# Attention values on 64x64 quarters of the matmul array, one query tile at a time, in a one-core attention and MLP kernel

## The chip, the cores and the metric

One core of a Trainium2 chip runs the whole program. The metric is the device time of one execution in microseconds (us). The kernel before took 914.94 us (median of three runs, 913.29 to 915.36).

## The reference, cut to what matters

```python
scores = scale * np.matmul(q, k.transpose(0, 1, 3, 2))      # q, k, v: 4 batches, 8 heads, 576 positions, 64 wide
psi_rel = np.log1p(np.abs(pos[:, None] - pos[None, :]))
psi_i = np.log1p(np.maximum(pos[:, None], 1.0))
h = np.maximum((psi_rel / psi_i)[..., None] @ w1 + b1, 0.0) # 32 hidden numbers for each pair of positions
scores = scores + (h @ w2).transpose(2, 0, 1)[None]         # one bias table per head, the same for all batches
attn = softmax(scores)
x = concatenated heads of np.matmul(attn, v)                # 4 x 576 x 512
...
x = two token and channel mixing MLPs of x                  # not touched by the change
```

Everything is fp32; the MLPs' weights and activations are split into two parts and multiplied in three terms.

## The kernel before, in words

The order on every engine is the order in which the program is written. The first 345 us are attention; the rest, the two MLPs, is not touched.

**Units.** `units` (lines 168 to 173) lists 80 units of work. A unit is one batch, one pair of heads and one tile of queries. Four tiles have 128 queries; the fifth, called the tail tile, has 64, and there both heads share one tile of 128 rows. Batch 0 comes first, by query tile (tail tile first); batches 1 to 3 follow, pair by pair.

**The loop** (line 659) is a pipeline over `n`. One turn issues, in this order: the scores of unit n+3 (`scores`, line 443, four 64x64 quarters of the array at once), the division by the softmax sums for unit n+2 (`normalise`, on POOL and DVE), the transposes of unit n (`turn`, line 510: tiles `x` and `y` for the 512 main keys of the two heads, and `z` for the 64 tail keys of both), in batch 0 the transpose of a query tile (`q_turn`) and the product of two groups of the bias table (`bias_product`), and late in the turn the values of unit n-1 (`values`, line 534). ACT copies `x` (line 516), takes one exp of unit n+3 (line 475), copies `z` (line 528) and takes the other exp; DVE adds the bias (`tensor_tensor_reduce`, line 464) and copies `y` (line 532).

**Values** (line 534) form, for one unit, the product of the transposed probabilities with v: eight matmuls of 128 rows by 64 columns of the array (two side by side, one for each head), then two 64x64 matmuls for the tail keys. The result lies in one PSUM bank, tag `o`; DVE copies it into `X` (`place`, line 436). For pairs 4 to 13 (`paired`, line 500) `values2` (line 556) takes two units of 128 queries together, 256 columns at a time, in two halves that stand in different turns; their transposed probabilities need a second set of buffers, which lies in room kept for later weights (`rooms`, lines 748 to 750).

**PSUM.** Eight banks: two tiles of two banks for scores and bias products (`s_tile`, line 328), and one bank each for the tags `x`, `y`, `z` and `o`.

**The front.** The bias table is made on the chip in 36 groups of 16 query rows, tail queries first (`groups`, line 169). A group is a DVE and ACT step (`hidden`, line 310), a matmul (`bias_product`, line 358), an ACT copy into `st` and a DMA that deals the rows out (`bias_place`, line 371). For main queries the 16 rows of a group go to every eighth partition of `bias_m`; for tail queries they go to 16 neighbouring partitions of `bias_t`, in two DMAs:

```python
D.dma_start(out=bias_m[i0 % P // 16:P:GT, i0 // P], in_=st)                  # line 381
D.dma_start(out=bias_t[a * TL + r0:a * TL + r0 + 16], in_=st[a:P:2])         # line 385
```

Main queries are therefore dealt over the partitions in the same way (`dealt`, `rows`, `place`); tail queries are not. All DMAs are issued by one queue, SP, in program order; `load_v` (line 251) is four of them for a pair of heads, and in batch 0 pairs 0 to 3 are loaded in turns -2 to 1 (`NV`, line 203).

Of the kernel before, what the change touches and what calls it, by code (L numbers as in the profile page):

```python
# [7 lines left out]
F32 = mybir.dt.float32  # L8
F32R = mybir.dt.float32r
I32 = mybir.dt.int32  # L10
AF = mybir.ActivationFunctionType
ALU = mybir.AluOpType
# [7 lines left out]
def kernel(ctx, tc, ins, consts, out, dbg=None, nb=4, stop=None):  # L20
    nc = tc.nc
    V, S, G, T, D = nc.vector, nc.scalar, nc.gpsimd, nc.tensor, nc.sync
# [3 lines left out]
    P = 128  # L26
# [173 lines left out]
    ND0, WN = 2, 512  # L200
    NQ = 2
    TD, QD = 1, 2
    NV = (-2, -1, 0, 1)
    zero = first.tile([P, N], F32, tag="st", name="zero", bufs=4)[:, 0:WN]
    V.memset(zero, 0.0)
    z0 = ps_t.tile([P, WN], F32, tag="x", name="z0")
# [164 lines left out]
    def bias_place(gi, ps):  # L371
        if gi in early:
            st = early.pop(gi)
        else:
            st = first.tile([P, N], F32, tag="st", name="bst", bufs=4)
        S.activation(
            out=st.rearrange("p (a n) -> p a n", a=2), in_=ps[:, :, 0:HN], func=AF.Identity, scale=1.0 / scale, bias=evb
        )
        i0 = 16 * gi
        if i0 < NM * P:  # L380
            D.dma_start(out=bias_m[i0 % P // 16:P:GT, i0 // P], in_=st)
        else:
            r0 = i0 - NM * P
            for a in range(2):
                D.dma_start(out=bias_t[a * TL + r0:a * TL + r0 + 16], in_=st[a:P:2])

    def k_parts0(p, pool, tag):

# [27 lines left out]
    def q_out(n, z):  # L416
        b, p, it = units[n]
        if b > 0:
            return
        w = P if it < NM else TL  # L420
        t = hl_p.tile([P, P], F32, tag="q0", name="q0", bufs=5)[:, 0:w]
        if it < NM:
            S.copy(out=rows(t), in_=dealt(z[:, 1]))
        else:
            S.copy(out=t, in_=z[:, 1, 0:w])
        queries[n] = t

    def dealt(x):  # L430
        return x.rearrange("p (t j s) -> p t s j", j=GT, s=P // GT)

    def rows(x):
        return x.rearrange("p (t s j) -> p t s j", j=GT, s=P // GT)

    def place(p, c0, o):

        V.tensor_copy(
            out=X[:, p, c0:c0 + o.shape[1]].rearrange("p (t j s) -> p t j s", j=GT, s=P // GT),
            in_=o.rearrange("p (t s j) -> p t j s", j=GT, s=P // GT),  # L440
        )

    def scores(n):
        b, p, it = units[n]
# [48 lines left out]
    def slots(flat):  # L493
        x, y, z = flat
        x, y = [t.rearrange("p (s t n) -> p s t n", s=2, t=NM) for t in (x, y)]
        return x, y, z.rearrange("p (s n) -> p s n", s=2)

    rooms = [slots(flatA)]

    def paired(n):  # L500

        return NP <= n // NS < len(pairs) - 2

    def room(n):
        if not paired(n):
            return rooms[0], n % 2
        it = units[n][2]
        return (rooms[0], it) if it < 2 else (rooms[1], 1 if it == NM else it - 2)

    def turn(n, pr, z):  # L510
        b, p, it = units[n]
# [22 lines left out]
    def values(n):  # L534
        b, p, it = units[n]
        vm, vt = vraw[b, p]
        (xs, ys, zs), s_ = room(n)
        xs, ys, zs = xs[:, s_], ys[:, s_], zs[:, s_]
        o = ps_t.tile([P, P], F32, tag="o", name="o")
        w = P if it < NM else TL  # L540
        for t in range(NM):
            T.matmul(o[0:HD, 0:w], lhsT=vm[:, t, 0], rhs=xs[:, t, 0:w], start=t == 0, stop=False)  # L542
            rh = ys[:, t] if it < NM else xs[:, t, TL:P]
            T.matmul(o[HD:P, 0:w], lhsT=vm[:, t, 1], rhs=rh, start=t == 0, stop=False)
        T.matmul(o[0:HD, 0:w], lhsT=vt[0:TL, 0], rhs=zs[0:TL, 0:w], start=False, stop=True)
        lh, rh = (vt[TL:P, 1], zs[TL:P]) if it < NM else (vt[0:TL, 1], zs[0:TL, TL:P])
        T.matmul(o[HD:P, 0:w], lhsT=lh, rhs=rh, start=False, stop=True)
        c0 = b * N + it * P
        if it < NM:
            place(p, c0, o)  # L550
        else:
            V.tensor_copy(out=X[:, p, c0:c0 + w], in_=o[:, 0:w])

    open_o = []

    def values2(n, half):

        b, p, it = units[n]
        vm, vt = vraw[b, p]
        xs, ys, zs = room(n)[0]  # L560
        if half == 0:
            open_o.append(ps_t.tile([P, 2 * P], F32, tag="o", name="o"))
        o = open_o[0]
        for t in range(2 * half, 2 * half + 2):
            T.matmul(o[0:HD], lhsT=vm[:, t, 0], rhs=xs[:, :, t], start=t == 0, stop=False)  # L565
            T.matmul(o[HD:P], lhsT=vm[:, t, 1], rhs=ys[:, :, t], start=t == 0, stop=False)
        if half == 0:
            return
        T.matmul(o[0:HD], lhsT=vt[0:TL, 0], rhs=zs[0:TL], start=False, stop=True)
        T.matmul(o[HD:P], lhsT=vt[TL:P, 1], rhs=zs[TL:P], start=False, stop=True)  # L570
        c0 = b * N + it * P
        place(p, c0, open_o.pop())


    early_v, late_v = {}, {}
    for n in range(U):
        if not paired(n):
            (early_v if n == U - 2 else late_v).setdefault(n + 1, []).append((values, n))
    for F in range(U0, U - 2 * NS, NS):
        late_v.setdefault(F + 2, []).append((values2, F, 0))  # L580
        late_v.setdefault(F + 3, []).append((values2, F, 1))
        early_v.setdefault(F + 4, []).append((values, F + 2))
        late_v.setdefault(F + 5, []).insert(0, (values2, F + 3, 0))
        late_v.setdefault(F + 5 if F + NS == U - 2 * NS else F + 6, []).insert(1, (values2, F + 3, 1))

    def form(l):
        for f, *a in l:
            f(*a)

    HP, TW = 1, 1  # L590
    GALL = len(groups)
    GUP = TL // 16 + 2
    hs = {}

    def hide(gi):
        if gi < GALL:
            hs[gi] = hidden(groups[gi])
# [25 lines left out]
            q_out(u, z)  # L623
    bias_place(groups[GUP - 1], bps)
    gnext = GUP

    def x_part(b, t, xs, px):

# [30 lines left out]
    for n in range(-3, U + 1):  # L659
# [7 lines left out]
            normalise(*st[n + 2])  # L667
        if len(gs) > 0:
            hide(gs[0] + 2)
        z = ps_t.tile([P, 2, P], F32, tag="z", name="z") if n < U else None  # L670
        form(early_v.pop(n, []))
        if n == U - 1:
            early_x([NM])
        if 0 <= n < U:
# [28 lines left out]
        for m in range(NP, len(pairs)):  # L703
            F = NS * m
            if n == F - KT:
                k_turn(*pairs[m])
            if n == F - QT:
                qt_, qr_, M = turned(*pairs[m]), qraw.pop(pairs[m]), NM * P
                V.transpose(
                    out=qt_[:, 0:M].rearrange("p (t s j) -> p t j s", j=GT, s=P // GT),  # L710
                    in_=qr_[:, 0:M].rearrange("p (t j s) -> p t j s", j=GT, s=P // GT),
                )
                V.transpose(out=qt_[:, M:N], in_=qr_[:, M:N])
        if len(gs) > 1:
            bias_place(groups[gs[1]], bp[1])
            if late_e:
# [10 lines left out]

        for p in range(NP):
            if n == NV[p]:
                load_v(0, p, *((raw_p, "") if p < 2 else (first, "x")))  # L730
        if n >= 0 and n % NP == 0 and n // NP + 2 < NS:
            load_q0(order0[n // NP + 2])
        for m in range(NP, len(pairs)):
# [7 lines left out]
        if n == U0:  # L741
            first.release()
            stg = tc.alloc_tile_pool(name="stg", bufs=1, side="right", reuse_waits="tile")
            tokw = tc.alloc_tile_pool(name="tokw", bufs=1, side="right", reuse_waits="tile")
            wjobs = Jobs(stg, 2)
            t1 = [tokw.tile([P, NS, TOK], F32R, name=f"t1{i}") for i in range(2)]

            rb = tokw.tile([P, 2 * NTT * N], F32, tag="t2", name="rb")
            cut = [0, 2 * NM * P, 4 * NM * P, 4 * NM * P + 2 * P]
            rooms.append(slots([rb[:, cut[i]:cut[i + 1]] for i in range(3)]))  # L750
            t2 = []
            for j in range(NM // 2):
                wjobs.add(
                    ("t1", j), "moe_w_tok1", slice(2 * j * P, (2 * j + 2) * P), slice(0, TOK), 2,
                    lambda j=j: [t[:, 2 * j:2 * j + 2, :] for t in t1],
                )
            wjobs.add(
                ("t1", NM // 2), "moe_w_tok1", slice(NM * P, N), slice(0, TOK), 1,
                lambda: [t[:, NM, :] for t in t1], 2,
            )  # L760
            for j in range(NTT):
                for hf in range(2):
                    js = slice(hf * HN, (hf + 1) * HN)
                    wjobs.add(
                        ("t2", j, hf), "moe_w_tok2", slice(j * P, (j + 1) * P), js, 1,
                        lambda j=j, js=js: [t[:, j, js] for t in t2],
                    )
            wjobs.load()
# [1 line left out]
            if wjobs.next <= NM // 2 or wjobs.gen is not None:  # L770
                wjobs.piece()
        if n == U - 2 * NS + 2:
            r = tokw.tile([P, 2, NTT, N], F32R, tag="t2", name="t2")
            t2 += [r[:, i] for i in range(2)]
        if n >= U - 2 * NS + 2:
            for _ in range(WP[1]):
# [573 lines left out]
```

## Time and profile before

| what | value |
|---|---|
| median of three runs | 914.94 us (913.29 to 915.36) |
| the profiled execution, its own time | 913.72 us |
| its span | 911.9 us |
| busy: TensorE, DVE, ACT, POOL | 894.5, 625.6, 394.0, 293.7 us |
[...]
| chain that ended last, by engine | TensorE 78%, DVE 16%, issue 2%, ACT 2%, DMA 2% |

Times in the rows count from the start of the span. PE is TensorE's matmuls and PEld its weight loads; an fp32 matmul shows as two passes, each with its own load, so the program's eight score matmuls are 16 rows. The mode of a matmul, as 64*64, is the piece of the array that it uses; pieces of one mode work at the same time. "idle before <-" gives how long the engine had stood and what ended it.

### The profile page before, as it was taken

Reading aid. Unit: us, or ns where it says so; the run is one execution under the profiler, and the core shown is the slowest. Engines: PE = TensorE matmul, PEld = TensorE weight load, DVE = VectorE, ACT = ScalarE, POOL = GpSimd, SP = SyncE. Lnnn points to the kernel's source line nnn. Section 1 sums busy time; section 2 is a strip of 40 time slices with the busy share of each in tenths; the row PEclk is TensorE's granted clock in tenths of the full one; section 3 lists DMA queues with packets and bytes.
Section 4 is the critical chain, followed back from the end, with each engine's and each line's share of the span. In section 5 each row is a group of like instructions: output and inputs, shape, how many; then the busy total and the mean of one; then the engine's idle time right before and its main releaser. Section 6 shows DMA issues by size and latency. Waiting matters only on the chain.

```text
span 911.9 us, 18151 instructions
## 1 busy us (share of the span) xinstructions
PE 894.5 (98%) x7018; PEld 749.8 (82%) x7018; DVE 625.6 (69%) x1371; ACT 394.0 (43%) x875; POOL 293.7 (32%) x430
## 2 busy tenths in 40 slices
PE   8799999999999999999999999999999999999998
PEld 3366776665666789899999999999999989889996
DVE  6799777887877769988834343232215999896756
ACT  6799766676666754433312121211114532222310
POOL 2366455555545532233310100100002452423230
PEclk9999999999999999999999999999999999999999
DMA  8775534333332113223400100000041001010002
GB/s 157 161 155 118 115 64 94 54 66 68 56 64 56 29 60 93 94 93 121 133 24 24 38 33 24 24 24 1 1 77 48 24 1 47 1 59 1 1 13 92
DMA packets 118966, 54.87 MB, mean 60 GB/s; under 512 B 100832, under 2 KB 107616, under 8 KB 118880
## 3 DMA queue, kind: packets, MB, share of 16 engines
q1 hardware_dynamic: 118880, 53.72, 24.7%
q8 instruction: 55, 0.90, 0.4%
q14 instruction: 31, 0.25, 0.1%
HBM read 38.36 MB, written 4.72 MB: 47 GB/s over the span
## 4 chain that ended last, share of the span: by engine, by line
PE 78%; DVE 16%; issue 2%; ACT 2%; DMA 2%; SPq 0%; DVEq 0%; ACTq 0%
PE a L985 14%; PE pg L822 14%; PE ss L456 9%; PE x L515 5%; PE o L565 4%; PE po L1202 4%; PE pv L1096 4%; PE ps L1171 4%; PE o L542 3%; PE y L520 3%; PE bps L363 3%; PE pu L1149 3%; DVE res L940 2%; DVE w L131 2%; PE pu L854 1%
## 5 line engine op out<-in xcount | busy, mean ns | idle before, releaser
L488 POOL TENSOR_SCALAR pr<-pr,sm 128x576 f32<-128x576 f32 (+2 forms) x208 | 129.1, 637 | 118.8 <-DVE sm L482 114.2
L985 PE MATMUL a<-g,c 128*128 128x384 f32 x864 | 162.4, 335 | 1.8 <-DVE X L993 1.0
L985 PEld LDWEIGHTS a<-g,c 128*128 128x128 f32 x864 | 150.9, 188 | 3.5 <-ACT g L828 2.2
L829 DVE SCALAR_TENSOR_TENSOR g<-pg,g 128x384 fp32r<-128x384 f32 x72 | 40.0, 556 | 163.7 <-ACT g L828 163.7
L822 PE MATMUL pg<-u,c 128*128 128x384 f32 x720 | 134.5, 334 | 0.0
L822 PEld LDWEIGHTS pg<-u,c 128*128 128x128 f32 x720 | 125.6, 188 | 0.1
L828 ACT ACTIVATE g<-pg 128x384 fp32r<-128x384 f32 x72 | 35.3, 490 | 192.2 <-PE pg L822 192.2
L475 ACT ACTIVATE pr<-pr,mn 128x576 f32<-128x576 f32 x144 | 112.0, 778 | 6.9 <-DVE mn L464 6.0
L464 DVE CUSTOM_DVE_ANT_0 pr<-ss,bias_m 128x576 f32<-128x576 f32 x128 | 91.3, 750 | 29.8 <-PE ss L456 29.2
L456 PE MATMUL ss<-kt,X 64*64 64x288 f32 x864 | 77.1, 412 | 0.0
L940 DVE STREAM_TRANSPOSE res<-X 32x256 f32<-32x256 f32 (+1 forms) x176 | 68.1, 387 | 2.8
L60 POOL TENSOR_TENSOR c<-w,c 128x512 fp32r<-128x512 f32 x24 | 35.5, 1479 | 88.9 <-ACT c L59 78.7
L60 POOL TENSOR_TENSOR wi<-w,wi 128x512 fp32r<-128x512 f32 x8 | 14.0, 1754 | 153.0 <-DVE g L829 112.5
L320 DVE TENSOR_SCALAR X<-ttab,wsm 128x576 f32<-128x576 f32 x108 | 62.3, 639 | 0.0
L515 PEld LDWEIGHTS x<-ident,pr 128*128 128x128 f32 x320 | 33.6, 141 | 30.4 <-POOL pr L488 18.9
L1171 PE MATMUL ps<-wsT,vn 128*128 128x288 f32 x384 | 56.5, 296 | 1.1 <-DVE tmp L1181 1.1
L456 PEld LDWEIGHTS ss<-kt,X 64*64 64x64 f32 x864 | 36.6, 132 | 22.3 <-DVE sm L482 7.3
L1171 PEld LDWEIGHTS ps<-wsT,vn 128*128 128x128 f32 x384 | 52.7, 189 | 1.9 <-DVE tmp L1181 1.8
L120 ACT ACTIVATE sq<-wraw 128x512 f32<-128x512 f32 (+2 forms) x43 | 27.9, 648 | 57.5 <-DVE w L136 56.3
L515 PE MATMUL x<-ident,pr 128*128 128x128 f32 x320 | 52.5, 286 | 0.0
L1149 PEld LDWEIGHTS pu<-y,wi 128*128 128x128 f32 x384 | 51.4, 188 | 0.3
L1149 PE MATMUL pu<-y,wi 128*128 128x288 f32 x384 | 51.6, 295 | 0.0
(188 smaller groups left out, 1760.0 us busy)
## 6 DMA issues: line engine op xcount, KB each, us to landing
wraw<-in_moe_w_ch_dram SPq DMA_DIRECT2D x24, 512.0 KB, 3.5
bias_m<-bst SPq DMA_DIRECT2D x32, 288.0 KB, 3.7
vm<-in_v_dram SPq DMA_DIRECT2D x32, 128.0 KB, 2.8
wraw<-in_moe_w_in_dram SPq DMA_DIRECT2D x8, 512.0 KB, 3.4
out_dram<-res SPq DMA_DIRECT2D x16, 256.0 KB, 2.0
kr<-in_k_dram SPq DMA_DIRECT2D x48, 72.0 KB, 2.4
qr<-in_q_dram SPq DMA_DIRECT2D x48, 72.0 KB, 2.4
wraw<-in_moe_w_out_dram SPq DMA_DIRECT2D x4, 512.0 KB, 3.6
```

The source lines that it names most:

```text
L60: (eng or V).tensor_tensor(out=lo, in0=src, in1=hi.bitcast(F32), op=ALU.subtract)
L320: V.tensor_scalar(out=hd, in0=tt, scalar1=b1i, scalar2=None, op0=ALU.min)
L456: T.matmul(ss[a % na][o, hf, 0:HN], lhsT=qt[r, m * HD:(m + 1) * HD], rhs=kt[r, js], start=True, stop=True)
L464: V.tensor_tensor_reduce(out=pr[:, a * NB:a * NB + N].rearrange("p (f n) -> p f n", f=2), in0=ss[a][:, :, 0:HN], in1=bias[a].rearrange("p ...
L475: S.activation(out=pr[:, a * NB:a * NB + N], in_=pr[:, a * NB:a * NB + N], func=AF.Exp, scale=-1.0, bias=mn[:, a:a + 1], accum_out=sm[:, a ...
L488: G.tensor_scalar(out=pr[:, dc:dc + hi - lo], in0=pr[:, lo:hi], scalar1=sm[:, a:a + 1], scalar2=1.0, op0=ALU.mult, op1=ALU.mult,)
L515: T.transpose(x[:, t], pr[:, t * P:(t + 1) * P], ident)
L822: T.matmul(pg, lhsT=c1[f][i][:, d], rhs=u[j][:, d], start=d == 0 and n == 0, stop=d == ND - 1 and n == 2)
L940: V.transpose(out=o, in_=src(c)[32 * a:32 * a + 32])
L985: T.matmul(acc[d], lhsT=c2[f][i][:, d * P:(d + 1) * P], rhs=g[j], start=f == f0 and n == 0, stop=f == f1 and n == 2,)
L1149: T.matmul(pu[:, hf, 0:HN], lhsT=wi[i][:, d, f * P:(f + 1) * P], rhs=y[j][:, d, js], start=d == 0 and m == 0, stop=d == ND - 1 and m == 2,)
L1171: T.matmul(ps[:, hf, 0:HN], lhsT=vn[i][:, t, ds_], rhs=wsT[j][:, t, js], start=t == 0 and m == 0, stop=False,)
```

## The change

It does six things. (1) `values` works on 64x64 quarters: each 128-row matmul is two of 64 rows, and the two halves of the rows add up in two PSUM banks, tag `o` and tag `z`, which is also the tag of the tail keys' transposes. (2) `place` adds the two banks: ACT copies the second into `X`, DVE adds the first. (3) `values2` and its second room go; every unit is formed alone. (4) From unit 11 on, the values of unit n-2 stand in turn n straight behind the scores of unit n+3, ahead of the transposes; up to unit 10 they stay late in the turn. The values of unit 78 follow those of unit 77 in turn 79. (5) Tail queries are dealt like main ones: the 16 rows of a group go to every fourth partition of `bias_t`. (6) In batch 0 v of pairs 0 and 1 is loaded ahead of the loop, that of pairs 2 and 3 in turns -3 and -2.

```diff
-    NV = (-2, -1, 0, 1)
+    NV = (None, None, -3, -2)
...
-                D.dma_start(out=bias_t[a * TL + r0:a * TL + r0 + 16], in_=st[a:P:2])
+                D.dma_start(out=bias_t[a * TL + r0 // 16:(a + 1) * TL:TL // 16], in_=st[a:P:2])
...
-    def place(p, c0, o):
-
-        V.tensor_copy(
-            out=X[:, p, c0:c0 + o.shape[1]].rearrange("p (t j s) -> p t j s", j=GT, s=P // GT),
-            in_=o.rearrange("p (t s j) -> p t j s", j=GT, s=P // GT),
-        )
+    def place(p, c0, os, w):
+
+        out = X[:, p, c0:c0 + w].rearrange("p (j s) -> p j s", s=16)
+        a, b = [o[:, 0:w].rearrange("p (s j) -> p j s", s=16) for o in os]
+        S.copy(out=out, in_=b)
+        V.tensor_tensor(out=out, in0=a, in1=out, op=ALU.add)
...
-        o = ps_t.tile([P, P], F32, tag="o", name="o")
...
+        os = [ps_t.tile([P, P], F32, tag=t, name="o") for t in "oz"]
         for t in range(NM):
...
+            for o, r in zip(os, halves):
+                T.matmul(o[0:HD, 0:w], lhsT=vm[r, t, 0], rhs=xs[r, t, 0:w], start=t == 0, stop=t == NM - 1 and o is os[1])
+                T.matmul(
+                    o[HD:P, 0:w], lhsT=vm[r, t, 1], rhs=rh[r], start=t == 0,
+                    stop=t == NM - 1 and (o is os[0]) == (it < NM),
+                )
...
+    GUP = TL // 16 + 2
+    early_v, late_v = {}, {}
+    BE = (len(groups) - GUP) // 2 - 4
+    for n in range(U):
+        if n == U - 2:
+            early_v.setdefault(n + 1, []).append((values, n))
+        elif n < BE or n == U - 1:
+            late_v.setdefault(n + 1, []).append((values, n))
         else:
...
+            early_v.setdefault(n + 2, []).insert(0, (values, n))
...
     bias_place(groups[GUP - 1], bps)
     gnext = GUP
+    for p in range(2):
+        load_v(0, p, raw_p, "")
...
+        form(early_v.pop(n, []))
         z = ps_t.tile([P, 2, P], F32, tag="z", name="z") if n < U else None
-        form(early_v.pop(n, []))
```

How the order moves, at three places.

TensorE, two turns of batches 1 to 3. Before (`x`, `y`, `z` are transposes, `ss` scores, L565 to L570 the paired values, here their second half):

```order
L520 MATMUL y<-ident,pr 128x128 [waits Pool_49]
L520 MATMUL y<-ident,pr 128x128 x3
L521 MATMUL z<-ident,pr 128x128 [waits Activation_49]
L565 MATMUL o<-xA,vm 64x256
L566 MATMUL o<-yA,vm 64x256
L565 MATMUL o<-xA,vm 64x256
L566 MATMUL o<-yA,vm 64x256
L569 MATMUL o<-zA,vt 64x256 [waits DMAHW2_49]
L570 MATMUL o<-zA,vt 64x256 [waits DMAHW3_49]
L456 MATMUL ss<-kt,X 64x288 [waits DVE_49]
```

and now (L535 and L536 are the values of the two heads; the third is the first that writes the second bank):

```order
L510 MATMUL y<-ident,pr 128x128 [waits DVE_49,Pool_49]
L510 MATMUL y<-ident,pr 128x128 x3
L511 MATMUL z<-ident,pr 128x128 [waits Activation_49]
L453 MATMUL ss<-kt,X 64x288 [waits DVE_49] x2
L453 MATMUL ss<-kt,X 64x288 x6
L535 MATMUL o<-xA,vm 64x128 [waits DVE_49]
L536 MATMUL o<-yA,vm 64x128
L535 MATMUL o<-xA,vm 64x128 [waits Activation_49]
L536 MATMUL o<-yA,vm 64x128
```

Values now follow scores instead of transposes, in the same mode, and their third matmul waits for ACT.

ACT, the same stretch. Before:

```order
L516 COPY xA<-x 128x512
L475 ACTIVATE pr,sm<-pr,mn 128x576
L528 COPY zA<-z 128x128
L475 ACTIVATE pr,sm<-pr,mn 128x576
L516 COPY xA<-x 128x512
```

and now:

```order
L437 COPY X<-o 128x128
L506 COPY xA<-x 128x512
L472 ACTIVATE pr,sm<-pr,mn 128x576
L518 COPY zA<-z 128x128
L472 ACTIVATE pr,sm<-pr,mn 128x576
L437 COPY X<-o 128x128
```

One copy out of the second bank is added per unit; the copy of `z` still stands behind the copy of `x` and one exp.

SP, the front. Before:

```order
L385 DMA bias_t<-early 16x4x576 x2
L381 DMA bias_m<-bst 16x8x576 x6
L255 DMA vm<-in_v_dram 128x4x64 x2
L259 DMA vt<-in_v_dram 64x2x64
L260 DMA vt<-in_v_dram 64x64
L381 DMA bias_m<-bst 16x8x576 x2
```

and now:

```order
L381 DMA bias_m<-bst 16x8x576 x2
L255 DMA vm<-in_v_dram 128x4x64 x2
L259 DMA vt<-in_v_dram 64x2x64
L260 DMA vt<-in_v_dram 64x64
L255 DMA vm<-in_v_dram 128x4x64 x2
L259 DMA vt<-in_v_dram 64x2x64
L260 DMA vt<-in_v_dram 64x64
L381 DMA bias_m<-bst 16x8x576 x2
```

All four loads of v now stand ahead of the last two of the first eight main groups; before, one did.

## Rows read from the trace of the kernel before

**Rows 1.** Busy time by stretch: PE, PEld, DVE, ACT, POOL; clock; DMA share, GB/s.

```profile
26.00:30.00 4.00, 3.73 (x24) 1.44 (x24) 2.80 (x8) 3.07 (x7) 0.35 (x1) 0.57 0.26 57
...
60.00:105.00 45.00, 44.86 (x621) 29.66 (x620) 41.67 (x99) 39.76 (x85) 27.50 (x46) 1.00 0.58 130
...
130.00:299.00 169.00, 169.00 (x1775) 104.07 (x1774) 129.82 (x348) 110.73 (x289) 90.23 (x186) 1.00 0.35 66
```

**Rows 2.** Chain that ended last, 14 to 46 us: start, length, what.

```profile
18.27 6.86 DMA bias_t<-early
...
38.09 5.08 DMA vm<-in_v_dram
```

**Rows 3.** Timeline of DVE, 19 to 46 us.

```profile
25.45 0.76 DVE L464 CUSTOM_DVE_ANT_0 pr<-ss,bias_t 128x576 f32<-128x576 f32 x1 [6.03 <-DMA bias_t<-early]
...
26.14 2.66 DVE L320 TENSOR_SCALAR X<-ttab,wsm 128x576 f32<-128x576 f32 x6
30.22 0.76 DVE L464 CUSTOM_DVE_ANT_0 pr<-ss,bias_t 128x576 f32<-128x576 f32 x1 [1.42 <-PE ss L456]
...
43.27 0.76 DVE L464 CUSTOM_DVE_ANT_0 pr<-ss,bias_m 128x576 f32<-128x576 f32 x1 [0.66 <-DMA vm<-in_v_dram]
```

**Rows 4.** Busy time by stretch, two stretches of DMA (columns as in rows 1).

```profile
17.00:23.00 6.00, 4.71 (x55) 1.97 (x47) 2.42 (x6) 4.13 (x9) 0.00 (x0) 1.00 1.06 135
34.00:36.00 2.00, 2.00 (x31) 1.05 (x32) 2.00 (x6) 1.57 (x5) 0.75 (x1) 1.00 1.02 258
```

**Rows 5.** DMA issues, 10 to 45 us: count, KB each, median us to landing.

```profile
bias_m<-bst SPq DMA_DIRECT2D x10, 288.0 KB, 4.1
...
bias_t<-early SPq DMA_DIRECT2D x4, 144.0 KB, 5.9
```

**Rows 6.** Timeline of SP, 15 to 41 us.

```profile
19.08 14.83 SPq L381 DMA_DIRECT2D bias_m<-bst  x6
33.97 1.21 SPq L255 DMA_DIRECT2D vm<-in_v_dram  x2
```

**Rows 7.** Timeline of PE, one unit with values of 128 columns.

```profile
115.51 0.66 PE L515 MATMUL x<-ident,pr 128*128 128x128 f32 x4
...
116.64 0.32 PE L542 MATMUL o<-xA,vm 128*64 128x128 f32 x1
...
116.80 0.27 PE L542 MATMUL o<-xA,vm 128*64 128x128 f32 x1
...
117.46 0.27 PE L542 MATMUL o<-xA,vm 128*64 128x128 f32 x1
...
117.66 0.32 PE L545 MATMUL o<-zA,vt 64*64 64x128 f32 x1
```

**Rows 8.** Timeline of PE, scores in quarters and the transposes behind them.

```profile
174.24 1.20 PE L456 MATMUL ss<-kt,X 64*64 64x288 f32 x16
175.37 0.33 PE L515 MATMUL x<-ident,pr 128*128 128x128 f32 x1
```

**Rows 9.** Timeline of 175.0 to 178.2 us: ACT behind those transposes.

```profile
176.06 0.59 ACT L516 COPY rb<-x 128x512 f32<-128x512 f32 x1 [0.52 <-PE x L515]
...
176.54 0.78 ACT L475 ACTIVATE pr<-pr,mn 128x576 f32<-128x576 f32 x1
...
177.31 0.25 ACT L528 COPY rb<-z 128x128 f32<-128x128 f32 x1
```

**Rows 10.** Timeline of ACT, 36.1 to 36.65 us.

```profile
36.04 0.74 ACT L376 ACTIVATE bst<-bps,evb 128x576 f32<-128x576 f32 x1
```

**Rows 11.** Timeline of PE, 36.1 to 37.0 us.

```profile
36.83 0.46 PE L456 MATMUL ss<-kt,q 64*64 64x288 f32 x2 [0.40 <-ACT bst L376]
```

**Rows 12.** Chain that ended last, 129 to 330 us: transposes of units 19 and 78.

```profile
129.55 0.59 PE x L515 x4
...
324.97 0.59 PE x L515 x4
```

**Rows 13.** Groups of instructions on DVE, 60 to 105 us: count, busy, mean ns, idle before.

```profile
L438 DVE COPY X<-o 128x128 f32<-128x128 f32 x7 | 2.0, 279 | 2.6 <-PE o L547 2.6
```

More of the change, by code (lines that the diff above doesn't have):

```diff
@@ L421, in q_out, with dealt, rows @@
         t = hl_p.tile([P, P], F32, tag="q0", name="q0", bufs=5)[:, 0:w]
[L422 to L425, printed above, removed]
+        S.copy(out=rows(t, w), in_=dealt(z[:, 1, 0:w], w))
         queries[n] = t
[L430 to L434, printed above, removed]
-    def place(p, c0, o):
-        V.tensor_copy(
-            out=X[:, p, c0:c0 + o.shape[1]].rearrange("p (t j s) -> p t j s", j=GT, s=P // GT),
-            in_=o.rearrange("p (t s j) -> p t j s", j=GT, s=P // GT),
-        )
+    def dealt(x, w=P):
+        return x.rearrange("p (t j s) -> p t s j", j=w // 16, s=16)
+    def rows(x, w=P):
+        return x.rearrange("p (t s j) -> p t s j", j=w // 16, s=16)
+    def place(p, c0, os, w):
[3 more added lines that the diff above has]
+        V.tensor_tensor(out=out, in0=a, in1=out, op=ALU.add)
     def scores(n):
@@ L498 @@
     rooms = [slots(flatA)]
-    def paired(n):
-        return NP <= n // NS < len(pairs) - 2
     def room(n):
[L505 to L508, printed above, removed]
+        return rooms[0], n % 2
     def turn(n, pr, z):
@@ L538, in values @@
         xs, ys, zs = xs[:, s_], ys[:, s_], zs[:, s_]
-        o = ps_t.tile([P, P], F32, tag="o", name="o")
         w = P if it < NM else TL
+        os = [ps_t.tile([P, P], F32, tag=t, name="o") for t in "oz"]
         for t in range(NM):
-            T.matmul(o[0:HD, 0:w], lhsT=vm[:, t, 0], rhs=xs[:, t, 0:w], start=t == 0, stop=False)
             rh = ys[:, t] if it < NM else xs[:, t, TL:P]
-            T.matmul(o[HD:P, 0:w], lhsT=vm[:, t, 1], rhs=rh, start=t == 0, stop=False)
-        T.matmul(o[0:HD, 0:w], lhsT=vt[0:TL, 0], rhs=zs[0:TL, 0:w], start=False, stop=True)
@@ L546, in values @@
-        lh, rh = (vt[TL:P, 1], zs[TL:P]) if it < NM else (vt[0:TL, 1], zs[0:TL, TL:P])
-        T.matmul(o[HD:P, 0:w], lhsT=lh, rhs=rh, start=False, stop=True)
-        c0 = b * N + it * P
-        if it < NM:
-            place(p, c0, o)
-        else:
[L552 to L572, printed above, removed]
@@ L575 @@
[L575 to L584, printed above, removed]
+            for o, r in zip(os, halves):
[4 more added lines that the diff above has]
+                )
@@ new lines, in values @@
+        T.matmul(os[0][0:HD, 0:w], lhsT=vt[0:TL, 0], rhs=zs[0:TL, 0:w], start=False, stop=True)
+        o, lh, rh = (os[1], vt[TL:P, 1], zs[TL:P]) if it < NM else (os[0], vt[0:TL, 1], zs[0:TL, TL:P])
+        T.matmul(o[HD:P, 0:w], lhsT=lh, rhs=rh, start=False, stop=True)
+        place(p, b * N + it * P, os, w)
+    GUP = TL // 16 + 2
[6 more added lines that the diff above has]
+            late_v.setdefault(n + 1, []).append((values, n))
+        else:
+            early_v.setdefault(n + 2, []).insert(0, (values, n))
@@ L591 @@
     GALL = len(groups)
-    GUP = TL // 16 + 2
     hs = {}
@@ L708 @@
                 qt_, qr_, M = turned(*pairs[m]), qraw.pop(pairs[m]), NM * P
[L709 to L713, printed above, removed]
+                for c, w in ((slice(0, M), P), (slice(M, N), TL)):
+                    V.transpose(
+                        out=qt_[:, c].rearrange("p (t s j) -> p t j s", j=w // 16, s=16),
+                        in_=qr_[:, c].rearrange("p (t j s) -> p t j s", j=w // 16, s=16),
+                    )
         if len(gs) > 1:
@@ L729 @@
             if n == NV[p]:
-                load_v(0, p, *((raw_p, "") if p < 2 else (first, "x")))
+                load_v(0, p, first, "x")
         if n >= 0 and n % NP == 0 and n // NP + 2 < NS:
@@ L746 @@
             t1 = [tokw.tile([P, NS, TOK], F32R, name=f"t1{i}") for i in range(2)]
-            rb = tokw.tile([P, 2 * NTT * N], F32, tag="t2", name="rb")
-            cut = [0, 2 * NM * P, 4 * NM * P, 4 * NM * P + 2 * P]
-            rooms.append(slots([rb[:, cut[i]:cut[i + 1]] for i in range(3)]))
             t2 = []
@@ L772 @@
         if n == U - 2 * NS + 2:
-            r = tokw.tile([P, 2, NTT, N], F32R, tag="t2", name="t2")
+            r = tokw.tile([P, 2, NTT, N], F32R, name="t2")
             t2 += [r[:, i] for i in range(2)]
```

## The prediction

> **What bounds the kernel now.** I read the busy time by stretch first, then the chain of waits, then the timelines of the places that the change touches. By stretches [rows 1], attention has three parts. From 130 to 299 us TensorE is busy for all 169.00 us, with DVE at 129.82 and ACT at 110.73: TensorE sets the pace. From 60 to 105 us, where the bias table is still made, TensorE (44.86 of 45), DVE (41.67) and ACT (39.76) are all nearly full. At the front they wait: the chain [rows 2] goes through a DMA into bias_t of 6.86 us, and DVE stands 6.03 us until 25.45 for it [rows 3]. [...]
>
> **The change part by part.** The sum is made against the profiled execution (913.72 us, 1.22 below the median 914.94) and then moved to the median.
>
> *Spread of bias_t.* From 17 to 23 us DMA is full (1.06) at 135 GB/s, and what moves is bias_t; from 34 to 36 us it is full (1.02) at 258 GB/s with bias_m [rows 4]. So 16 rows on 16 neighbouring partitions go at half the rate of 16 rows on every eighth; a DMA of 144 KB takes longer to land (5.9 us) than one of 288 (4.1) [rows 5]. The rate on every fourth partition is in no row; it lies between the two, and I take 258, because every fourth spreads the rows like every eighth and not like neighbours. The last six of the eight DMAs, 0.88 MB, then take 3.4 us instead of 6.6, and the last lands near 22.0 instead of 25.13: 3.2 us. [...]
>
> [...]
>
> *v loaded early.* All sixteen issues of v on SP now stand ahead of the last main groups, twelve more than before. Two took 1.21 us, so a pair's four take some 2.5 [rows 6]. The first two pairs fill time in which SP waited for ACT (six issues in 14.83 us) [rows 6]. What pays is the first bias_m: from 19.08 SP now has 8 group and 16 v issues, 24 x 0.62 = 14.9 us, to 34.0, plus 4.1 to land [rows 5]: 38.1. [...] What then follows, to 105 us, is bound by DVE, and carries the gain.
>
> *Units 0 to 10, values late.* DVE's copy (279 ns [rows 13]) becomes an add of the same shape, which I price alike; ahead of it DVE now waits for ACT's copy of the second bank, some 0.25 us by the copy of z [rows 9]. TensorE saves a change of mode, but DVE is as full. Nothing to 0.25 x 11 = 2.8 us; I take +0.3, since ACT has that copy's inputs before DVE is through with its hidden layers.
>
> *The turn from unit 19 to 78.* First TensorE alone. From the first transpose to the next work in another mode is 1.13 us (115.51 to 116.64) [rows 7]. Scores take 1.13 up to the transposes (174.24 to 175.37) [rows 8]. A change of mode costs 0.20 - 0.11 = 0.09: 117.46 to 117.66 against a pass every 0.11 (116.80 to 117.46 in six steps) [rows 7]; with values right behind, scores take 1.04. Quarters do the same work per pass (four at once instead of two twice as tall): ten passes, eight and two for the tail keys, 1.10, plus 0.09. Sum 3.36 us per unit, against 195.42 us for 59 units (129.55 to 324.97 [rows 12]), 3.31 on average with the paired values. Eleven turns transpose a tail tile (0.44 less) and eleven form values of 64 columns (0.55 less, by half-length passes), and the last two have no scores (1.04 less): 59 x 3.36 - 4.8 - 6.1 - 2.1 = 185.3 us, 10.1 less than before.
>
> But the second bank is handed on late. The values of turn n may write tag z only when ACT has copied z of turn n-1, and ACT does that behind its copy of x and an exp: from the first transpose at 175.37 to the end of the copy of z, 177.56, are 2.19 us [rows 8, 9]. TensorE goes on 0.05 later, as at 36.83 behind ACT's end at 36.78 [rows 10, 11], and its first pass costs 0.05 more (116.64 to 116.80 is 0.16 against 0.11 [rows 7]). So a turn cannot be shorter than 2.24 + 0.05 + 1.19 = 3.48 us, and 2.86 where the values have 64 columns. That is 0.12 above TensorE's own 3.36, and in the eleven turns of a tail tile, whose scores come 0.44 earlier, 0.56 above. 47 x 3.48 + 11 x 2.86 + 2.7 (no exp in the last) = 197.7 us: **+2.3**. ACT is then what ends TensorE's wait before the third value matmul; DVE has slack (129.82 of 169), and ACT's added 0.25 us per unit too.
>
> [...]
>
> *The end.* Values of unit 78 follow those of unit 77 and need both banks emptied: an ACT copy and a DVE add one after the other, about 0.6 us, less the change of mode saved: +0.5. *Units 11 to 18* wait for the copy of a query tile behind z as well, in three turns: +0.1. The dealt tail tiles move the same elements: nothing.
>
> **Sum:** -4.6 + 0.3 + 0.1 + 2.3 + 0.5 = -1.4 us: 912.3 for the profiled execution, **913.5** for the median.
>
> **Rivals.**
> *A, the forecast* (46%): 910 to 917, from a front gain of 3.0 to 5.5 and 0.05 us per turn either way (2.7).
> *B, TensorE keeps the pace* (18%). If z is copied sooner than I read, each tenth of a us per turn is 5.9 us over 59 turns, down to 914.94 - 4.6 + 0.4 - 10.1 + 0.5 = 901. For it: TensorE has no gap now. Against: the third value matmul waits for ACT.
> *C, slower: the loop over ACT is longer* (20%). ACT's copy of the second bank stands ahead of its copy of x. Its input ends 0.07 us after x starts (0.27 long, 0.20 before) and x ends at 0.66, so the copy, 0.05 + 0.25, has 0.3 us to spare; an exp or a weight conversion that runs late uses it up and lengthens the loop. It costs the whole gain at a turn of 3.51 us (1.4 / 47 above 3.48), and from 3.55 us on the kernel is slower by over 0.2%; at 3.60 it is 913.5 + 47 x 0.12 = 919. For it: three engines now hand two banks to one another. Against: ACT is busy for two thirds.
> *D, the spread does not do what it says* (16%): rows every fourth partition still go at 135 GB/s, or v pushes bias_m back. Then the front gives 0 to 2: 916 to 918.
>
> **How the numbers follow.** 0.2%, 1.8 us, is about what a measurement of this kernel tells from no change: 913.1 to 916.8. A lies across the edge: 23 faster, 21 same, 2 slower. B is faster (18), C slower (17) or same (3), D half and half (8 and 8). Faster 0.41, same 0.32, slower 0.27. The range 907 to 918.5 leaves out two thirds of B and some of C.
>
> **What would show it.** Right: the first bias addition starts near 22, with no stretch at 0.57 of the clock, the one with bias_m near 38; transposes of full units 3.45 to 3.5 us apart, with ACT's copy of z as what ended TensorE's stand at the values, and 59 turns in 196 to 199 us. Wrong: turns of 3.36 and 59 of them in some 185 us (B), turns over 3.55 (C), bias_t still landing near 25 (D).

## The result, and the profile after

The changed kernel took **925.13 us** (median of four runs, 922.5 to 925.51) against 915.15 for the kernel before: 1.0107 times as long (95% interval 1.0093 to 1.012). The forecast was 913.5, in a range of 907 to 918.5: the kernel became slower, and its time lies outside. The profiled execution took 924.85 us, its span is 923.1 (911.9 before).

Where the 11.2 us came in is read from the starts of the transposes of units 12, 19 and 78 and of the last transposes behind attention. TensorE's timeline of the changed kernel:

```profile
107.06 0.44 PE L505 MATMUL x<-ident,pr 128*128 128x128 f32 x2
...
132.52 0.44 PE L505 MATMUL x<-ident,pr 128*128 128x128 f32 x2
...
334.50 0.44 PE L505 MATMUL x<-ident,pr 128*128 128x128 f32 x2
...
350.48 0.38 PE L604 MATMUL px<-ident,X 128*128 128x128 f32 x2
```

and of the kernel before, where units 19 and 78 are in [rows 12] (the chain's starts there are 0.07 later than the timeline's):

```profile
104.70 0.66 PE L515 MATMUL x<-ident,pr 128*128 128x128 f32 x4
...
339.34 0.49 PE L632 MATMUL px<-ident,X 128*128 128x128 f32 x3
```

| stretch | before | after | difference | forecast |
|---|---|---|---|---|
| start to unit 12 | 104.70 | 107.06 | +2.36 | -4.3 |
| unit 12 to 19 | 24.78 | 25.46 | +0.68 | +0.1 |
| unit 19 to 78 | 195.42 | 201.98 | +6.56 | +2.3 |
| unit 78 to the end of attention | 14.44 | 15.98 | +1.54 | +0.5 |

So two terms carry the miss, and both hold a wait. **The front.** DVE's bias additions in the changed kernel, which answer to [rows 3]:

```profile
22.18 0.76 DVE L461 CUSTOM_DVE_ANT_0 pr<-ss,bias_t 128x576 f32<-128x576 f32 x1 [3.10 <-PE bps L363]
...
25.88 0.76 DVE L461 CUSTOM_DVE_ANT_0 pr<-ss,bias_t 128x576 f32<-128x576 f32 x1 [0.35 <-PE ss L453]
...
43.27 0.76 DVE L461 CUSTOM_DVE_ANT_0 pr<-ss,bias_m 128x576 f32<-128x576 f32 x1 [5.08 <-DMA bias_m<-bst]
```

The first two come 3.27 and 4.34 us earlier. The first that needs `bias_m` starts at 43.27 as before, with 5.08 us of waiting in place of 0.66: DVE was through with its other work at 38.19. The chain that ended last has the DMA, SP's timeline the issues ahead of it:

```profile
36.10 6.85 DMA bias_m<-bst
```

```profile
20.05 1.20 SPq L381 DMA_DIRECT2D bias_m<-bst  x2
21.29 1.55 SPq L255 DMA_DIRECT2D vm<-in_v_dram  x2
...
35.44 4.18 SPq L381 DMA_DIRECT2D bias_m<-bst  x4
```

The eighth main group is issued at 36.10 and lands at 42.95. Meanwhile the DMA engines are full (a share of 1.04 from 30 to 42 us), and then TensorE, which stood too, has a granted clock of 0.50 (42 to 46 us; 1.00 there in the kernel before). Busy time by stretch (columns as in [rows 1]), and TensorE's first bias products after the stand:

```profile
26.00:30.00 4.00, 3.81 (x48) 1.85 (x50) 4.00 (x10) 3.87 (x8) 2.70 (x4) 1.00 0.76 185
30.00:42.00 12.00, 9.36 (x100) 4.74 (x92) 8.18 (x18) 9.02 (x18) 4.72 (x8) 0.93 1.04 204
42.00:46.00 4.00, 1.82 (x16) 0.92 (x17) 2.73 (x8) 1.18 (x4) 1.12 (x1) 0.50 0.57 81
...
130.00:299.00 169.00, 167.23 (x2887) 130.32 (x2887) 129.14 (x356) 118.94 (x330) 86.53 (x180) 1.00 0.36 69
```

```profile
44.18 3.63 PE L363 MATMUL bps<-X,w2q 128*32 128x288 f32 x32 [2.52 <-DVE mn L461]
51.25 2.19 PE L363 MATMUL bps<-X,w2q 128*32 128x288 f32 x32 [0.54 <-DVE mn L461]
```

The first of these products starts at 44.18 in the kernel before too, but there it takes 2.18 us, and the next transposes start at 48.34; here they start at 49.83. That is 1.49 of the 2.36 us that are lost by unit 12; for units 0 to 10 the run early_one_bank, below, finds 0.87.

**The turn.** A full turn takes 3.55 us, a turn with values of 64 columns 2.93. One of them on TensorE (first transpose, first value matmul, third one, next transpose) and on ACT:

```profile
174.12 0.66 PE L505 MATMUL x<-ident,pr 128*128 128x128 f32 x4
...
176.28 0.27 PE L535 MATMUL o<-xA,vm 64*64 64x128 f32 x1
...
176.43 0.32 PE L535 MATMUL o<-xA,vm 64*64 64x128 f32 x1
...
177.67 0.55 PE L505 MATMUL x<-ident,pr 128*128 128x128 f32 x3
```

```profile
174.23 0.27 ACT L437 COPY X<-o 128x128 f32<-128x128 f32 x1 [0.63 <-PE o L542]
174.87 0.59 ACT L506 COPY xA<-x 128x512 f32<-128x512 f32 x1 [0.37 <-PE x L505]
175.35 0.78 ACT L472 ACTIVATE pr<-pr,mn 128x576 f32<-128x576 f32 x1
...
176.12 0.26 ACT L518 COPY zA<-z 128x128 f32<-128x128 f32 x1
```

ACT ends the copy of `z` at 176.38, and the third value matmul, the first into the second bank, follows at 176.43. Its quarter is not the first two's, so that it could have run beside them from 176.3, as in a turn without this wait, where the matmuls to all four quarters start together (104.84 to 104.86 us). The list of waits names it too, where TensorE shows a gap at all (mostly the turns of a tail tile):

```profile
PE o L535 <- ACT zA L518: 2.6, 12, 0.5
```

### The profile page after: what moved, and what is told of

Its sections match the earlier page's. It is cut to its first block, busy times and chain, and to the rows that moved or that the text cites. A ratio compares the mean times of both kernels' runs of the same rounds, so it can differ in the third digit from the quotient of the medians.

```text
span 923.1 us, 21654 instructions
## 1 busy us (share of the span) xinstructions
PE 899.4 (97%) x8698; PEld 786.5 (85%) x8698; DVE 629.8 (68%) x1391; ACT 411.8 (45%) x955; POOL 293.5 (32%) x430
## 4 chain that ended last, share of the span: by engine, by line
PE 74%; DVE 16%; ACT 4%; issue 3%; DMA 1%; POOL 0%; DVEq 0%; SPq 0%; ACTq 0%
PE a L953 14%; PE pg L790 14%; PE ss L453 7%; PE o L535 7%; PE x L505 5%; PE po L1170 4%; PE pv L1064 4%; PE ps L1139 3%; PE bps L363 3%; PE pu L1117 3%; PE y L510 3%; DVE res L908 2%; DVE w L131 2%; ACT pr L472 2%; DVE w L136 1%
## 5 line engine op out<-in xcount | busy, mean ns | idle before, releaser
L535 PEld LDWEIGHTS o<-xA,vm 64*64 64x64 f32 x1280 | 80.1, 133 | 25.2 <-ACT zA L518 6.0
L535 PE MATMUL o<-xA,vm 64*64 64x128 f32 (+1 forms) x1280 | 94.1, 264 | 3.5 <-ACT zA L518 2.6
L536 PE MATMUL o<-yA,vm 64*64 64x128 f32 x1024 | 81.4, 274 | 0.0
L453 PE MATMUL ss<-kt,X 64*64 64x288 f32 x864 | 71.9, 415 | 0.0
L536 PEld LDWEIGHTS o<-yA,vm 64*64 64x64 f32 x1024 | 68.1, 132 | 0.0
L506 ACT COPY xA<-x 128x512 f32<-128x512 f32 x80 | 46.8, 585 | 26.9 <-PE x L505 26.9
L522 DVE COPY yA<-y 128x512 f32<-128x512 f32 x64 | 44.0, 688 | 16.7 <-PE y L510 16.0
```

The source lines that it names most:

```text
L453: T.matmul(ss[a % na][o, hf, 0:HN], lhsT=qt[r, m * HD:(m + 1) * HD], rhs=kt[r, js], start=True, stop=True)
L535: T.matmul(o[0:HD, 0:w], lhsT=vm[r, t, 0], rhs=xs[r, t, 0:w], start=t == 0, stop=t == NM - 1 and o is os[1])
L536: T.matmul(o[HD:P, 0:w], lhsT=vm[r, t, 1], rhs=rh[r], start=t == 0, stop=t == NM - 1 and (o is os[0]) == (it < NM),)
```

## The experiments

The theory: the whole loss is v ahead of `bias_m` at the front, the late hand-over of tag `z` in the turns, and the adjacent values of units 77 and 78 at the end; quarters and spread are gains. First, one part undone or mended at a time.

**v_as_before**, the change without part (6):

```diff
-    NV = (None, None, -3, -2)
+    NV = (-2, -1, 0, 1)
...
-    for p in range(2):
-        load_v(0, p, raw_p, "")
...
```

> The change with only part (6) undone: v of pairs 0 to 3 is loaded in turns -2 to 1 again. Theory: in the changed kernel the first bias addition from bias_m stands 5.08 us for a DMA of 6.85 us, because 0.9 MB of v go ahead of it; and TensorE's clock falls while it stands. Without them that addition starts near 38.5 instead of 43.27, the clock keeps its level, the transposes of unit 12 start near 100.5 (107.06 with the change, 104.70 before), and the time is 925.1 - 6.5 = 918.6 (917 to 920). Rival, that the new deal of bias_t (neighbouring rows every fourth partition) is what holds bias_m back: the addition stays near 43 and the time within 1 us of 925.

Measured: 919.09 us, 1.0052 (1.0031 to 1.0072) of before, 6.0 us less than the change, as expected. The profiled execution, 922.3, is the slowest of its four and was late from the start (first bias addition at 24.13). So its rows are not the expected ones: the addition with `bias_m` starts at 42.33 and not near 38.5, and the clock is 0.60 from 26 to 30 us. But of DVE's wait of 5.08 us there 1.20 are left:

```profile
42.33 0.76 DVE L461 CUSTOM_DVE_ANT_0 pr<-ss,bias_m 128x576 f32<-128x576 f32 x1 [1.20 <-PE z L412]
```

**z_first**, the change with ACT's copy of `z` moved ahead of the first exp (line 472) from turn 11 on, and the copy of the query tile with it:

```diff
-        if 0 <= n + 3 < U:
+        if 0 <= n + 3 < U and n < BE:
             softmax(*st[n + 3], which=(0,))
...
             z_out(z, zs, y)
...
             q_out(n + 5, z)
+        if n >= BE and n + 3 < U:
+            softmax(*st[n + 3], which=(0,))
```

> The change, with ACT copying z (and the query tile) ahead of the first exp from turn 11 on; nothing else. Theory: the 6.5 us that units 19 to 78 lost against before (201.98 us for 59 turns against 195.42) are the late hand-over of tag z; with it gone, full turns go from 3.55 us to 3.36 to 3.40 and the 59 turns take 186 to 190 us: 925.1 - 13 = 912 (909 to 914). Rival, that the quarters themselves or the first pass after each change cost TensorE the time: turns stay over 3.5 and the time within 2 us of 925. Second rival, that the exps, now later, hold up POOL and the transposes: a new wait ahead of the transposes, turns between.

Measured: **907.45 us**, 0.9925 (0.9906 to 0.9944) of before, and less than the 909 to 914 that were expected. ACT, and TensorE's transposes of units 19 and 78:

```profile
174.83 0.59 ACT L506 COPY xA<-x 128x512 f32<-128x512 f32 x1 [0.38 <-PE x L505]
175.32 0.27 ACT L518 COPY zA<-z 128x128 f32<-128x128 f32 x1
175.49 0.78 ACT L472 ACTIVATE pr<-pr,mn 128x576 f32<-128x576 f32 x1
```

```profile
129.41 0.44 PE L505 MATMUL x<-ident,pr 128*128 128x128 f32 x2
...
316.62 0.55 PE L505 MATMUL x<-ident,pr 128*128 128x128 f32 x3
```

The copy of `z` ends at 175.59, before the scores do. Full turns take 3.36 us, the 59 turns 187.21: 14.8 less than in the change, and 8.2 less than before. Both rivals fall: the quarters are not slow, and the later exps hold nothing up. Units 12 to 19 give another 1.3; the rest of the 17.7 lies ahead of unit 12 (its transposes start at 105.23 and not 107.06), where nothing was changed, and is the spread between executions. In this one of the same front DVE's wait is shorter too:

```profile
41.58 0.76 DVE L461 CUSTOM_DVE_ANT_0 pr<-ss,bias_m 128x576 f32<-128x576 f32 x1 [3.96 <-issue]
```

**v_z_end**, both together, and the values of unit 77 late in turn 78:

```diff
-        elif n < BE or n == U - 1:
+        elif n < BE or n in (U - 3, U - 1):
```

> Both of these, and the values of unit 77 again late in turn 78 (not next to those of unit 78). Theory: the three parts add up, 6.5 + 13 + 1.3 us: 925.1 - 20.8 = 904.3 (902 to 908), faster than both kernels. Rival: the front's gain is taken up by DVE or ACT before unit 19, and the time stays over 909.

Measured: **902.76 us**, 0.9866 (0.9851 to 0.988). The 59 turns take 187.20 again, and from unit 78 to the end of attention it is 14.98 us instead of 15.98. Against z_first the time is 4.7 less, 1.0 of it at the end; so v is worth 3.7 us by this pair and 6.0 by v_as_before. In the profiled executions 3.93 us less of DVE's wait than in the change (1.15 for 5.08) brought unit 12 forward by 5.42 (101.64 for 107.06). Where DVE waits for `bias_m`, and TensorE's first two pieces of work after its stand at the front:

```profile
39.47 0.76 DVE L461 CUSTOM_DVE_ANT_0 pr<-ss,bias_m 128x576 f32<-128x576 f32 x1 [1.15 <-PE x L505]
```

```profile
23.14 1.20 PE L363 MATMUL bps<-X,yA 128*32 128x288 f32 x16 [1.35 <-DVE mn L461]
24.78 1.19 PE L453 MATMUL ss<-kt,q 64*64 64x288 f32 x8 [0.44 <-ACT bst L376]
```

**spread_only**, the kernel before with part (5) alone (the line of the change for `bias_t`, and the tail tile's queries dealt to match):

```diff
-                D.dma_start(out=bias_t[a * TL + r0:a * TL + r0 + 16], in_=st[a:P:2])
+                D.dma_start(out=bias_t[a * TL + r0 // 16:(a + 1) * TL:TL // 16], in_=st[a:P:2])
```

> The kernel before with part (5) alone: the rows of a tail group go to every fourth partition of bias_t and tail queries are dealt to match; v, values and everything else as before. Theory: the gain that was forecast for this part is real: the first bias addition near 22, the second near 26, and from the one with bias_m on 4 to 5 us earlier than before: 915.15 - 4.6 = 910.5 (909.5 to 912). Rival: the bias_m deals, which now start while other transfers are under way, land no earlier and the time is 914 to 916.

Measured: 911.61 us, 0.9959 (0.9946 to 0.9972): 3.7 less than before. Its profiled execution (912.4, the slowest of its runs) does not have the expected rows: the first addition is at 24.17 and not near 22, the one with `bias_m` at 41.84, only 1.4 us earlier than before. The stand at the front was longer than in v_z_end, and the same scores took nearly twice as long:

```profile
24.99 1.20 PE L363 MATMUL bps<-X,yA 128*32 128x288 f32 x16 [2.20 <-DVE mn L461]
26.64 2.15 PE L453 MATMUL ss<-kt,q 64*64 64x288 f32 x8 [0.44 <-ACT bst L376]
```

**no_spread**, v_z_end with part (5) alone undone, the two lines of the last diff the other way round.

> The kernel of the third run with part (5) alone undone: the rows of a tail group go to 16 neighbouring partitions of bias_t again. Theory: the spread is worth here what it is worth in the kernel before, 3.7 us: 902.8 + 3.7 = 906.5 (905 to 908), with the first bias addition near 25.5 and the clock down from 26 to 30 us. Rival: with v and the values as they are there, something else holds the front, and the time is 902.5 to 904.

Measured: 907.63 us, 0.9926 (0.9909 to 0.9942), 4.9 above v_z_end. DVE's first addition, and the clock of 26 to 30 us:

```profile
26.48 0.76 DVE L467 CUSTOM_DVE_ANT_0 pr<-ss,bias_t 128x576 f32<-128x576 f32 x1 [6.46 <-DMA bias_t<-early]
```

```profile
26.00:30.00 4.00, 2.69 (x20) 1.02 (x22) 3.35 (x8) 2.04 (x5) 0.35 (x1) 0.50 0.30 57
```

So, by the times, the spread is worth 3.7 us in the kernel before and 4.9 in v_z_end. What was wrong with v, SP's issues or the bytes, was then told apart by **v_quarter**, the change with its sixteen early issues kept, and three quarters of their rows loaded later:

```diff
-    def load_v(b, p, pool, tag):
+    def load_v(b, p, pool, tag, ts=slice(0, NM)):
...
-                out=m[:, :, a], in_=v[b, 2 * p + a, 0:NM * P, :].rearrange("(t p) d -> p t d", p=P)
+                out=m[:, ts, a],
+                in_=v[b, 2 * p + a, ts.start * P:ts.stop * P, :].rearrange("(t p) d -> p t d", p=P),
...
-        load_v(0, p, raw_p, "")
+        load_v(0, p, raw_p, "", slice(0, 1))
...
-                load_v(0, p, first, "x")
+                load_v(0, p, first, "x", slice(0, 1))
+            if n == p - 1:
+                load_v(0, p, None, "", slice(1, NM))
```

> The changed kernel with as many early issues of v as it has (sixteen on SP, in the same places), but each load of the main keys brings only the first quarter of its rows there; the other three quarters come in turns -1 to 2, behind the eighth main group. So SP's time is kept, and the bytes ahead of bias_m fall from 1.2 MB to 0.45 MB. Theory: of the 5.08 us that DVE stood before its first addition from bias_m, about half were the DMA engines' time for v's bytes (the last main group took 6.85 us to land, 4.1 in the kernel before) and half SP's issues: that addition starts near 40.5 instead of 43.27 and the time is 921.5 (920 to 923). Rival, SP alone: it starts near 42.5, 924.5. Rival, bytes alone: near 38.8, 919.5.

Measured: 921.85 us, 1.0072 (1.0051 to 1.0094). DVE, the chain and SP:

```profile
40.78 0.76 DVE L467 CUSTOM_DVE_ANT_0 pr<-ss,bias_m 128x576 f32<-128x576 f32 x1 [2.51 <-issue]
```

```profile
36.38 1.46 DMA bias_m<-bst
```

```profile
35.71 1.24 SPq L387 DMA_DIRECT2D bias_m<-bst  x2
```

and SP in v_later, the next run, which has no v ahead of the eighth main group:

```profile
20.00 13.51 SPq L381 DMA_DIRECT2D bias_m<-bst  x8
```

5.08 became 2.51, and from the issue of the eighth main group to the addition it is 4.40 us (36.38 to 40.78) instead of 7.17 (36.10 to 43.27): about half is the bytes. The other half is mostly SP: the issue of that group is over at 36.95 here, and at 33.51 in v_later. The profile names nothing that ended these 2.51 us, and z_first, with all of v's bytes, had 6.00 (35.58 to 41.58); so the halves are rough, from one execution each.

**v_later** takes v_z_end and loads v one turn later still, `NV = (-1, 0, 1, 2)`.

> The kernel of the third run (v in turns -2 to 1, z ahead of the exp, values of unit 77 late) with v one turn later still, in turns -1 to 2: now none of it stands ahead of the eighth main group on SP. Theory: each pair of v ahead of that group, 0.3 MB, puts the first bias addition from bias_m off; the 1.15 us that DVE still stood there go, and nothing of v comes too late for its values: 902.8 - 1.1 = 901.7 (901 to 902.5). Rival: the wait there is DVE's on TensorE or SP's own pace, and the time stays at 902.8; or v now lands late and the values wait: over 903.5.

Measured: 902.09 us, 0.9867 (0.9852 to 0.9882). DVE's wait falls to 0.54, as expected, and nothing waits for v, but against before the time cannot be told from v_z_end's: 0.7 us is less than these runs tell apart.

```profile
38.68 0.76 DVE L461 CUSTOM_DVE_ANT_0 pr<-ss,bias_m 128x576 f32<-128x576 f32 x1 [0.54 <-ACT X L322]
```

**early_one_bank** adds the values of before for units 0 to 10:

```diff
+        if n < BE:
+            o = ps_t.tile([P, P], F32, tag="o", name="o")
...
+            return
         os = [ps_t.tile([P, P], F32, tag=t, name="o") for t in "oz"]
```

> The kernel with v one turn later, and for units 0 to 10, while the bias table is made, the values of before: 128 rows by 64 columns in one bank, copied by DVE alone. Theory: in those turns DVE waits up to 0.31 us per unit for ACT's copy of the second bank, and from the transposes of unit 0 to those of unit 12 the kernel takes 67.98 us against 66.63 with the values of before: about 1.3 us less, 900.4 (899.5 to 901.5). Rival, that ACT and DVE are full there by the bias table alone: no change.

Measured: 901.74 us, 0.9859 (0.9845 to 0.9874). That is above the 899.5 to 901.5 that were expected. From unit 0 to unit 12 it takes 66.63 us where v_later takes 67.50. So the step is worth 0.87, not 1.3 (that came from v_z_end, whose 67.98 still held a wait for `bias_m`), and by time it can't be told from v_later.

**ends_one_bank** does the same for units 77 to 79 (`n < BE or n >= U - 3`).

> The fastest kernel so far (z ahead of the exp, v in turns -1 to 2, one bank for units 0 to 10), with the values of before (128 rows by 64 columns, one bank) for units 77 to 79 too. Theory: there TensorE stands 0.41, 0.22 and 0.53 us for a bank; from the transposes of unit 78 to the third ones after them it takes 14.98 us against 14.44 with the values of before: 901.7 - 0.5 = 901.2 (900.7 to 901.8). Rival: those waits are DVE's and ACT's own lateness with the MLP's first tiles, and stay: 901.7.

Measured: **901.0 us**, 0.9849 (0.9833 to 0.9865), the least of all. From unit 78 to the end of attention it is 14.45 us instead of 14.98, as forecast; again the time alone does not tell it from the one before it. Against the kernel before, v_z_end and the three versions built on it are faster by 12 to 14 us.

## Why the prediction was wrong

**What bounds the kernel** was read rightly: TensorE sets the pace from 130 to 299 us (busy for 169.00 us before, for 167.23 now), and what it waits for there is the result.

**Spread of bias_t: right.** First addition 22.18 (near 22 was said), the gain at the second 4.34 (4.6 was said), the clock 1.00 from 26 to 30 us. From 14 to 18 us of the changed kernel, where five of these DMAs are issued, 211 GB/s move with the DMA engines 0.83 busy: by proportion an estimated 254 at full share, where 258 was taken. That is an estimated 1.9 times the 135 of [rows 4] for 16 neighbours. No run shows the -4.6 us of the sum, nor the 3.0 and 5.5 between which rival A has it: they were the author's estimates. In their place the runs showed the 4.34, and by the times 3.7 us (spread_only) and 4.9 (no_spread against v_z_end).

**v loaded early: the step that failed at the front.** "38.1" for the eighth main group is 42.95, for two reasons. SP's 24 issues began at 20.05 and not 19.08, and followed each other every 0.70 us, waits included, and not 0.62, so that the last began at 36.1, when all were to be over at 34.0. And the landing was taken as the 4.1 us of [rows 5], the median of ten that run from 3.1 to 7.5 us: it is 6.85 behind v's bytes. Bytes over rate would have warned of it: the three more pairs of v, 0.9 MB, at the 204 GB/s of 30 to 42 us are an estimated 4.4 us. v_quarter shows the two halves, roughly. And the wait was priced as if it only ate the gain. Behind it TensorE also ran at a granted clock of 0.50: 3.63 us for a product of 2.19. Rival D had "v pushes bias_m back", but with 0 to 2 us left of the gain; by unit 12, with the 0.87 of units 0 to 10, the whole gain was gone and 2.36 more.

**Units 0 to 10:** +0.3 was said between 0 and 2.8; it is 0.87. **Units 11 to 18:** +0.1 was said; it is 0.68, and -0.60 with the copy of `z` moved up (24.18 us from unit 12 to 19 in z_first), so the late hand-over costs there too.

**The turn: the mechanism was right, and its size off.** Three terms held: TensorE 0.05 behind ACT (176.38 to 176.43), 1.24 us from there to the next transpose (0.05 + 1.19), and TensorE's own 3.36, which z_first shows. What failed is the 2.19 from the first transpose to the end of the copy of `z`: it is 2.26, for the copy of `x` starts 0.75 behind the first transpose and not 0.69. The kernel before had that number too, in the very turn of [rows 7]; its ACT, behind the transposes at 115.51:

```profile
116.26 0.59 ACT L516 COPY xA<-x 128x512 f32<-128x512 f32 x1 [1.16 <-PE x L515]
...
117.51 0.26 ACT L528 COPY zA<-z 128x128 f32<-128x128 f32 x1
```

115.51 to 117.77 is 2.26. In the order of instructions this copy waits for two semaphores, TensorE's and one of ACT itself, as those of the change's full turns do; the one in [rows 9], out of the paired units, waits for TensorE's alone. From 111 to 176.1 us of the kernel before, the 13 copies of the first kind start 0.74 to 0.76 us behind the first transpose, the 7 others 0.69 to 0.70. That the second wait is what costs the 0.06 was not tried. 0.07 us over 58 turns is 4.1 of the 4.3 that the 59 turns are over the forecast's 197.7. (The forecast's 2.86 for values of 64 columns is not what its own terms give: 3.48 less its 0.55 is 2.93. Half of the 1.24 behind ACT's copy gives 2.86, and the trace bears that half out, 149.30 to 149.92 us; with the 0.07 it makes the measured 2.93.) So rival C's turn, 3.55, came true, but not by C's mechanism: ACT's copy of the second bank ended at 174.50, and ACT then stood 0.37 us for TensorE.

TensorE does wait for a copy out of PSUM (2.6 us in 12 waits that the list shows), and the 59 turns take 201.98 us; but with the same copy one exp earlier they take 187.2 (185.3 was said for TensorE alone), so it is the place of the copy in ACT's order that costs, not its length (0.26 us in the change, 0.27 in z_first).

**The end:** +0.5 was said for two copies; it is 1.54. TensorE waited twice:

```profile
337.54 1.25 PE L604 MATMUL px<-ident,X 128*128 128x128 f32 x8 [0.97 <-DVE bias_m L60]
...
340.73 0.32 PE L535 MATMUL o<-xA,vm 64*64 64x128 f32 x1 [0.68 <-DVE X L438]
```

The first wait is for DVE's work on the first MLP tile; in the kernel before, the values of unit 77 stood in that place (326.90 us), and the forecast left their going out. The second is for DVE's addition of unit 77, which came behind the MLP's tiles. With unit 77 back in turn 78 the stretch takes 14.98, with one bank 14.45.

Mended, the same ideas give what rival B was priced at, 901 us, but not part by part: B's turns were to gain 10.1 us, and 8.2 came.

## What to carry to other kernels

When a bank gets a second user, its hand-over becomes a loop over another engine's program order: follow it through that engine's queue with the slowest row of each kind, and look first for a copy that can be moved up; here one copy moved ahead of an exp was worth 15 us. Price a transfer that is moved ahead of a needed one by its bytes and by its issues on the queue: here each was roughly half of the 5.08 us that DVE waited (2.51 in v_quarter). TensorE's granted clock was down as well after the stand (0.50 from 42 to 46 us), and 3.9 us of added wait put unit 12 off by 5.4.

## What the runs showed of the hardware

Not expected was how sharply the front's cost goes with TensorE's stand there. After stands of 1.35 us (v_z_end) and 1.61 (the change) the next eight score matmuls took 1.19 us, at a granted clock of 1.00 from 26 to 30 us; after 2.20 (spread_only) and 2.14 (v_as_before) 2.15 and 2.18, at one of 0.59 and 0.60. Between v_z_end and v_as_before, two executions of one front, 1.81 us at the first bias addition (22.32 and 24.13) became 2.80 at the second (26.02 and 28.82). No run changed the stand alone; that the stand lowers the clock was not shown.
